# Layer-norm statistics on another engine, seven skip terms taken early, and two B tiles by transposing loads, in a one-core S5 and MLP mixer

## The chip, the cores and the metric

The kernel runs on one core of a Trainium2 chip. A time is device microseconds from launch to end of one execution. An execution that is profiled also has a span: the time from its first to its last instruction, in which the profile places everything. Kernels are compared by their medians.

A core has five engines that each work through a queue of their own in order[...]: TensorE (PE in the profile; its weight loads are shown apart as PEld), VectorE (DVE), ScalarE (ACT), GpSimd (POOL) and SyncE (SP). In this kernel SP issues loads and all transposing DMAs, POOL issues stores and accumulating DMAs.

## The reference

Input x has 2048 rows (time) of 1024 columns, in bfloat16. Cut to what matters:

```python
g = _sigmoid((x * gate_w).sum(-1, keepdims=True))
# A: a diagonal complex state space model, 1024 states
Bu = einsum("bld,pd->blp", x, B_bar)              # B_bar complex, rows p
h[t] = Lam_bar * h[t-1] + Bu[t]
a = 2.0 * einsum("blp,dp->bld", h, Cmat).real + x * Dskip
# B: layer norm, then an MLP with 3584 hidden units
y = (x - mean(x)) / sqrt(var(x) + 1e-5)
b = gelu(y @ w1 + b1) @ w2 + b2
return g * a + (1 - g) * b
```

The term of the skip that the change touches is g * x * Dskip; the statistics that it touches are the mean and the variance of each row of x.

## The kernel before

**Stages.** PE goes through four kinds of work. First the start: the first x rows and the B rows of p tiles 0 and 1 (a p tile is 128 of the 1024 states) are transposed on PE and multiplied plainly. Then the B stage, Bu: fourteen groups of 28 matmuls of 512 columns, each a block product of two by two blocks that takes seven block products in place of eight (class SG; its parts p1 to p7 are the seven products, with sums of operands made by DVE and sums of results made by ACT and DVE). Then the MLP in eight blocks: "m" blocks (x W1 and gelu, seven groups each) and "b" blocks (times W2, four groups each), over two halves of the hidden units (Fh) and two halves of the rows (c), in the order m00 b00 m01 b01 m11 b11 m10 b10. Last the y stage: eight groups of 56 matmuls, states times C, in the order of row blocks 4 5 6 0 1 2 3 7, with the final sum.

The MLP's result of the half Fh = 0 goes, already scaled by (1 - g), to a scratch tensor ACS in DRAM, one piece of 128x1024 f32 per tile k of 128 rows (L1459, a store on POOL). That of Fh = 1 is added to it by an accumulating DMA (L1461, on POOL). The y stage loads the piece back (L1527).

The state scans (L1238 to L1265, function ssm) lie on DVE beside the MLP, as work of low priority; their results go through DRAM (HS) to the y stage.

**What sets the order.** The program adds tasks to a graph with an engine, an estimated duration and a priority (small is early). A list scheduler simulates the engines with these estimates and writes down each engine's queue. A task is held back in this plan until its operands are there by the estimates: a result handed to another engine costs 0.2 us, data from a DMA 3 us more before a compute engine uses it, and a task may have further slack (the attribute slack). On the chip each engine follows the written order, waiting at each instruction for what it needs. So a change of any estimate or priority can reorder queues everywhere.

**What the change touches.**

- B rows of p tiles 2 and 3: load_b (L626 to L637) loads them plainly on SP; t_b (L657 to L678) transposes them on PE, eight transposes (L666) for each of the real and imaginary part, into PSUM, and ACT copies them out (L677). bu_plain (L963 to L983) calls t_b for tile 2 between the matmuls of tile 1, row chunk 0, and for tile 3 between those of tile 0, row chunk 1 (its argument mid). B rows of p tiles 4 to 7 come by transposing DMAs on SP already (bT_dma, L1146 to L1150). Their transposing loads must have landed before the first four stores of Bu to DRAM (u_store, L958, POOL): us_t's tasks get them as dependencies.
- x columns by row chunk of 512 rows, as PE needs them: chunk 0 is transposed on PE, chunks 1 to 3 by transposing DMAs on SP (xT_dma, L1048).
- The gate's row sums: z_gate (L1108 to L1125) multiplies all of x by two columns, gate_w and ones, in 32 matmuls (L1116), ACT copies the result out (L1124), z_move stores it (L1132, POOL) and loads it back by columns (SP). The columns are Z, for the gate, and SUM, for the means. It is called after p3 of the first group of the B stage. It must come before the fourth sum of x (ut4 of x_sums), which overwrites x chunk 1 with what p4 of that group needs.
- Layer-norm statistics: ln_stats (L1068 to L1095), called once per four tiles of 128 rows. ACT squares each tile and sums along the row (L1072); POOL computes mean, mean of squares, square of the mean, variance, its power -1/2 and mean times that (L1082 to L1087) on 128x4 columns; DVE normalizes each tile in place (L1092); the rows are stored to DRAM (L1094) and come back transposed (L1061).
- Skip terms: in the y stage y_load (L1512 to L1531) loads, for each of the 16 tiles, ACS[k] (L1527) and x (L1528) on SP; DVE multiplies x by Dskip (L1529, 128x1024 bf16) and adds g times that to the ACS piece (L1530, 128x1024 f32).
- Eviction buffers of Bu: EVS, and EVN, which gives the buffer of each of the fourteen groups.

The helper dve_tt (L940) records most two-operand additions, mm (L876 with start, L878 without) records the groups' matmuls, snap and begin (L895, L896, L905) and the seed in p1 (L912) record ACT's copies from PSUM. A seed copies the bank of p1 to the bank in which p6 goes on; between p1 and p6 lie p7 of the group before and p5.

Of the kernel before, what the change touches and what calls it, by code (L numbers as in the profile page):

```python
# [7 lines left out]
F32 = mybir.dt.float32  # L8
# [31 lines left out]
def c_tt16(N):  # L40
    return 0.07 + N / 1920.0
# [378 lines left out]
def build(nc, A_x, A_Lambda_re, A_Lambda_im, A_B_re, A_B_im, A_C_re, A_C_im, A_log_dt, A_Dskip,  # L420
# [25 lines left out]
    with es:  # L446
# [14 lines left out]

        NCOL = 660
        CST = sb("cst", [128, NCOL], F32)
# [90 lines left out]
        b_cst["MS0"] = bc("S1")  # L554
        alloc_cols("MHALF", TT)
        alloc_cols("KF", 2 * PT)
# [24 lines left out]
        def bcast(ap, off, name):  # L581
# [11 lines left out]
              reads=[v_ones], writes=[b_ident], name="ident")  # L593
        g.add("pool", 0.3, P0, lambda e: e.memset(C("MHALF", 0, TT), -0.5), writes=[bc("MHALF")], name="mhalf")

# [348 lines left out]
        b_hs = [[B("hs%d_%d" % (p, h)) for h in range(L // T)] for p in range(PT // 4)]  # L944
        EVS = [EV0, EV0 + 4096, BQ[2], SSM, SSM + 4096, SSM + 8192]
        us_t = {}
        xpose_t = {}
        EVN = (0, 1, 0, 1, 0, 1, 2, 0, 5, 1, 2, 0, 1, 2)
        US5 = B2B
# [12 lines left out]

        def bu_plain(pt, c, mid=None):  # L963

# [3 lines left out]
            for ri in range(2):  # L968
# [11 lines left out]
                if c % 2 == 1:  # L980
                    u_store(pt, c // 2, ks, q, ri)
                if mid is not None:
                    t_b(mid, (1.0, q), (ri,), (7, 3), pe_last)  # L983

# [82 lines left out]

        def ln_stats(c, prio):  # L1068
            for i in range(TT):
                k = c * TT + i  # L1070
                xv = XNAT[k]
                g.add("act", c_act(D, psum=False) + 0.15, (max(prio[0], 4.0), k), lambda e, xv=xv, k=k: e.activation(v_j.ap, xv.ap, AF.Square, accum_out=C("SSQ", k)),  # L1072
                      reads=[xv], writes=[v_j, bc("SSQ%d" % k)], name="ln_sq%d" % k, extra=[first_a[3]])
            k0 = c * TT

            def po(nm, fn, rd, wr):
                g.add("pool", 0.5, prio, fn, reads=[bc(r) for r in rd], writes=[bc(w) for w in wr], name="ln_%s%d" % (nm, c))
            invD = 1.0 / D
            sums = ["SUM%d" % (k0 + i) for i in range(TT)]
            sqs = ["SSQ%d" % (k0 + i) for i in range(TT)]  # L1080
            s = ".%d" % c
            po("mean", lambda e: e.tensor_scalar(C("MEAN", k0, TT), C("SUM", k0, TT), invD, 0.0, ALU.mult, ALU.add), sums, ["MEAN" + s])  # L1082
            po("ex2", lambda e: e.tensor_scalar(C("EX2", k0, TT), C("SSQ", k0, TT), invD, 1e-5, ALU.mult, ALU.add), sqs, ["EX2" + s])  # L1083
            po("msq", lambda e: e.tensor_tensor(C("MSQ", k0, TT), C("MEAN", k0, TT), C("MEAN", k0, TT), ALU.mult), ["MEAN" + s], ["MSQ" + s])
            po("var", lambda e: e.tensor_tensor(C("VAR", k0, TT), C("EX2", k0, TT), C("MSQ", k0, TT), ALU.subtract), ["EX2" + s, "MSQ" + s], ["VAR" + s])
            po("rstd", lambda e: e.tensor_tensor(C("RSTD", k0, TT), C("VAR", k0, TT), C("MHALF", 0, TT), ALU.pow), ["VAR" + s, "MHALF"], ["RSTD" + s])
            po("nmr", lambda e: e.tensor_tensor(C("NMR", k0, TT), C("MEAN", k0, TT), C("RSTD", k0, TT), ALU.mult), ["MEAN" + s, "RSTD" + s], ["NMR" + s])  # L1087
            for i in range(TT):
                k = k0 + i
                xv = XNAT[k]  # L1090
                o = xv
                g.add("dve", 0.35, prio, lambda e, xv=xv, k=k, o=o: e.tensor_scalar(o.ap, xv.ap, C("RSTD", k), C("NMR", k), ALU.mult, ALU.subtract),  # L1092
                      reads=[xv, bc("RSTD" + s), bc("NMR" + s)], writes=[o], name="ln_norm%d" % k)
                g.dma(prio, lambda e, k=k, o=o: e.dma_start(out=XNS[k * 128:(k + 1) * 128, :], in_=o.ap), 128 * D * 2,  # L1094
                      ssem("xns", k, True), reads=[o], writes=[b_xns[k]], name="xns%d" % k, q="sp" if k < 8 else "pool", extra=xn_t if k > 7 else ())  # L1095
# [31 lines left out]
        def z_move():  # L1127
# [8 lines left out]
            def em_ld(e):  # L1136
                return [e.dma_start(out=C(("Z", "SUM")[r], 0, NTT), in_=bass.AP(ZS.tensor, ZS.offset + r * L, [[1, 128], [128, NTT]]), allow_slow_non_contiguous=True) for r in range(2)]
            g.dma(prio, em_ld, L * 8, sem("d_zl"), reads=[b_zs[0]], writes=[bc("Z%d" % k) for k in range(NTT)] + [bc("SUM%d" % k) for k in range(NTT)], name="zl", ndma=2)

        xT_dma(1, (-0.84, 0))  # L1140
        load_b(2, (-0.83, 0))
        load_b(3, (-0.82, 0))
        xT_dma(2, (-0.4, 0))
        xT_dma(3, (-0.3, 0))

        def bT_dma(pt):  # L1146
            for ri, ap in enumerate((A_B_re, A_B_im)):
                o = AR.v(bqo(pt, 2 * ri), [(128, DT), (1, 128)])
                xpose_t[pt, ri] = g.dma((0.3, pt, ri), lambda e, o=o, ap=ap, pt=pt: e.dma_start_transpose(out=o.ap, in_=ap[pt * 128:(pt + 1) * 128, :]), 128 * D * 2,
                      ssem("bT", 2 * pt + ri), writes=[o], name="bTd%d.%d" % (pt, ri), xpose=True)  # L1150

        for c in range(2):
            for pt in range(2):
                bu_plain(pt, c, {(1, 0): 2, (0, 1): 3}.get((pt, c)))
        for k in range(4, 8):
# [11 lines left out]
        for n, (pt, pr) in enumerate(order):  # L1167
# [10 lines left out]
            cur.p6()  # L1178
            cur.p2()
            cur.p3()  # L1180
            if n == 0:
                z_gate()
                z_move()
                x_sums(0, seq[0], (1,))
                for c in range(2):
                    ln_stats(c, (2.55, c))
            if prev is not None:
# [14 lines left out]
        pb[0] = 10.0  # L1202
        for c in range(2, NCH):
            ln_stats(c, (4.0, c))

# [169 lines left out]


        HF = FT // 4

# [43 lines left out]
        def b_group(Fh, c, tp):  # L1422
# [19 lines left out]
            def fin(qd, q, bk):  # L1442
# [13 lines left out]
                if done.get(2 * t) and done.get(2 * t + 1):  # L1456
                    av = AR.v(o0[t], [(1, D)], F32)
                    if Fh == 0:
                        g.dma((10.0, q + 2), lambda e: e.dma_start(out=ACS[k], in_=av.ap), 128 * D * 4, ssem("ao", k % 4, True), reads=[av], writes=[b_acs[k]], name="acs%d.%d" % (Fh, k), q="pool")  # L1459
# [52 lines left out]
        def y_load(yi, ts=(0, 1), state=True):  # L1512
# [8 lines left out]
            for t in ts:  # L1521
                n = 2 * yi + t
                k = 2 * qb + t
                av = AR.v(AV[n % 8], [(1, D)], F32)
                xi = 0 if n < 1 else 1 + n % 4
                xv = AR.v(XV[xi], [(1, D)])
                g.dma((52.0, n), lambda e, av=av, k=k: e.dma_start(out=av.ap, in_=ACS[k]), 128 * D * 4, ssem("yac", n % 8), reads=[b_acs[k]], writes=[av], name="acl%d" % k)  # L1527
                g.dma((52.0, n), lambda e, xv=xv, k=k: e.dma_start(out=xv.ap, in_=x2[k * 128:(k + 1) * 128, :]), 128 * D * 2, ssem("yx", xi), writes=[xv], name="yx%d" % k)  # L1528
# [75 lines left out]
        for n, it in enumerate(flat):  # L1604
# [33 lines left out]
            if prev is not None:  # L1638
# [7 lines left out]
                elif kind == "m":  # L1646
                    w1_due[0] += x > 0
            if kind == "b":
                if w1_due[0]:
# [110 lines left out]
```

## Time and profile before

| | |
|---|---|
| median of 8 runs | 562.19 us (560.14 to 565.11) |
| the profiled execution | 560.14 us, the fastest of the eight |
| its span | 558.4 us |
| mean granted TensorE clock | 0.997 of full speed |
| chain that ended last, by engine | PE 87%, DVE 3%, ACT 2%, issue 2%, SP's queue 2%, POOL 1%, DMA 1% |
| moved by DMA | 125.58 MB, mean 225 GB/s |
| transposing loads of B rows (L1149) | 8, 256 KB each, 1.2 to 1.9 us of SP, 4.1 to 5.7 us from issue to landing |
| transposing loads of x (L1048) | 3, 1 MB each, 4.3 to 6.7 us of SP, 6.5 to 10.4 us from issue to landing |
| statistics on POOL (L1082 to L1087) | 24 instructions on 128x4 f32, 0.19 to 3.84 us each |
| skip terms on DVE in the y stage (L1529, L1530) | 16 tiles, mean 685 and 1278 ns |

A row of a timeline or of a group names line, engine and operation, what is written from what is read, shapes and count; brackets hold the idle time of the engine just before and what ended it. A mean duration of a pipelined engine is longer than the distance of its instructions: 512-column matmuls show 379 ns and follow one another every 216 ns; products of 128x1024 on DVE show 685 ns and follow every 600.

### The profile page before, as it was taken

Reading aid. Unit: us, or ns where it says so; the run is one execution under the profiler, and the core shown is the slowest. Engines: PE = TensorE matmul, PEld = TensorE weight load, DVE = VectorE, ACT = ScalarE, POOL = GpSimd, SP = SyncE. Lnnn points to the kernel's source line nnn. Section 1 sums busy time; section 2 is a strip of 40 time slices with the busy share of each in tenths; the row PEclk is TensorE's granted clock in tenths of the full one; section 3 lists DMA queues with packets and bytes.
Section 4 is the critical chain, followed back from the end, with each engine's and each line's share of the span. In section 5 each row is a group of like instructions: output and inputs, shape, how many; then the busy total and the mean of one; then the engine's idle time right before and its main releaser. Section 6 shows DMA issues by size and latency. Waiting matters only on the chain.

```text
span 558.4 us, 7447 instructions
## 1 busy us (share of the span) xinstructions
PE 543.4 (97%) x2576; PEld 250.2 (45%) x2623; DVE 520.2 (93%) x897; ACT 284.5 (51%) x477; POOL 101.6 (18%) x152
## 2 busy tenths in 40 slices
PE   8999999999999999999999999999999999999995
PEld 6444444444444444444444444444444444444442
DVE  3899999999999999999999999999999998999852
ACT  3998897657764356764346662347663231111110
POOL 2027916750001010001120101120001110011000
PEclk9999999999999999999999999999999999999998
DMA  9999889758757363315999997897688799898501
GB/s 249 278 199 285 294 193 306 261 185 257 226 121 263 115 225 114 109 41 163 336 343 325 333 252 197 204 228 246 199 235 166 168 309 352 286 356 307 176 38 56
DMA packets 122758, 125.58 MB, mean 225 GB/s; under 512 B 70475, under 2 KB 99929, under 8 KB 121697
## 3 DMA queue, kind: packets, MB, share of 16 engines
q1 hardware_dynamic: 110256, 79.33, 50.4%
q0 software_dynamic: 12464, 45.78, 26.3%
q8 instruction: 20, 0.33, 0.2%
q14 instruction: 18, 0.14, 0.1%
HBM read 60.98 MB, written 48.38 MB: 196 GB/s over the span
## 4 chain that ended last, share of the span: by engine, by line
PE 87%; DVE 3%; ACT 2%; issue 2%; SPq 2%; POOL 1%; DMA 1%; DVEq 0%; POOLq 0%; ACTq 0%
PE ps L878 66%; PE ps L876 20%; SPq L1048 1%; DVE ar L1252 1%; DMA ar<-in_A_B_im_dram 1%; DVE ar L940 1%; ACT ar L1072 1%; ACT ar L677 0%; DVE ar L1238 0%; POOL scr_u L958 0%; DVE ar L1370 0%; POOL cst L1083 0%; DVE ar L1039 0%; PE ps L1116 0%; DVE ar L1092 0%
## 5 line engine op out<-in xcount | busy, mean ns | idle before, releaser
L878 PE MATMUL ps<-ar 128*128 128x512 f16 (+1 forms) x1793 | 411.7, 379 | 3.3 <-ACT ps L912 1.2
L878 PEld LDWEIGHTS ps<-ar 128*128 128x128 f16 (+1 forms) x1832 | 178.9, 98 | 218.4 <-ACT ps L912 3.0
L940 DVE TENSOR_TENSOR ar<-ar 128x512 f16<-128x512 bf16 (+7 forms) x244 | 149.7, 653 | 5.7 <-ACT ar L677 2.1
L876 PE MATMUL ps<-ar 128*128 128x512 bf16 (+1 forms) x616 | 152.2, 379 | 1.7 <-DVE ar L940 1.1
L876 PEld LDWEIGHTS ps<-ar 128*128 128x128 bf16 (+1 forms) x624 | 60.6, 98 | 74.1 <-DVE ar L940 1.6
L1252 DVE TENSOR_TENSOR_SCAN ar<-cst,init,ar 128x256 bf16<-128x256 f32 x128 | 88.3, 735 | 0.4
L895 ACT ACTIVATE ar<-ps 128x512 f32<-128x512 f32 x100 | 59.1, 596 | 47.8 <-PE ps L876 35.4
L1238 DVE TENSOR_TENSOR ar<-ar 128x2048 bf16<-128x2048 bf16 x64 | 77.0, 1218 | 0.1
L912 ACT ACTIVATE ps<-ps 128x512 f32<-128x512 f32 x66 | 38.5, 583 | 66.1 <-PE ps L876 54.7
L1366 ACT ACTIVATE ar<-ps,cst 128x512 bf16<-128x512 f32 x56 | 38.4, 686 | 22.8 <-PE ps L878 22.2
L896 ACT ACTIVATE ar<-ps,cst 128x512 f32<-128x512 f32 x32 | 22.0, 688 | 44.6 <-PE ps L878 19.9
L1372 ACT ACTIVATE ar<-ar,cst 128x512 bf16<-128x512 f32 x56 | 40.0, 714 | 7.9 <-DVE ar L1370 7.9
L1449 ACT ACTIVATE ar<-ps,cst 128x512 f32<-128x512 f32 x32 | 22.0, 688 | 40.8 <-PE ps L878 40.7
L1241 DVE TENSOR_TENSOR ar<-ar 128x1024 bf16<-128x1024 bf16 x64 | 42.6, 685 | 0.1
L1370 DVE TENSOR_TENSOR ar<-ps,ar 128x512 f32<-128x512 f32 x56 | 38.3, 684 | 2.8 <-PE ps L878 2.4
L958 POOL DMA_DIRECT2D scr_u<-ar x32 | 25.0, 785 | 29.3 <-DVE ar L1034 19.0
L1551 DVE SCALAR_TENSOR_TENSOR ar<-ps,cst,ar 128x512 bf16<-128x512 f32 x32 | 23.6, 747 | 7.1 <-PE ps L878 7.0
L1459 POOL DMA_DIRECT2D scr_ac<-ar x16 | 8.6, 535 | 113.4 <-DVE ar L1452 62.6
L1461 POOL DMA_DIRECT2D scr_ac<-ar x16 | 13.8, 871 | 82.2 <-DVE ar L1452 40.8
L1452 DVE SCALAR_TENSOR_TENSOR ar<-ps,cst,ar 128x512 f32<-128x512 f32 x32 | 23.7, 742 | 1.1 <-PE ps L878 0.9
L1270 POOL DMA_DIRECT2D scr_h<-ar x16 | 9.1, 569 | 81.1 <-DVE ar L1241 74.4
L1558 POOL DMA_DIRECT2D out_dram<-ar x14 | 7.6, 546 | 82.9 <-DVE ar L1551 82.9
(118 smaller groups left out, 269.7 us busy)
## 6 DMA issues: line engine op xcount, KB each, us to landing
scr_ac<-ar POOLq DMA_DIRECT2D x32, 512.0 KB, 6.0
ar<-in_B_w_dram SPq DMA_DIRECT2D x21, 512.0 KB, 5.2
ar<-in_A_x_dram SPq DMA_DIRECT2D x32, 256.0 KB, 4.8
scr_u<-ar POOLq DMA_DIRECT2D x32, 256.0 KB, 4.8
ar<-scr_u SPq DMA_DIRECT2D x16, 512.0 KB, 4.7
scr_h<-ar POOLq DMA_DIRECT2D x16, 512.0 KB, 5.9
ar<-scr_h SPq DMA_DIRECT2D x8, 1024.0 KB, 7.9
ar<-scr_ac SPq DMA_DIRECT2D x16, 512.0 KB, 7.5
```

The lines of the kernel that those rows point to most:

```text
L876: ins = e.matmul(V(PS[bk], 0, [(1, n)]), st[i].ap, mv[i].ap, start=(i == 0), stop=(i == K - 1))
L878: ins = e.matmul(V(PS[bk], 0, [(1, n)]), st[i].ap, mv[i].ap, start=False, stop=(i == K - 1), skip_group_check=True)
L895: return e.activation(o.ap, V(PS[bk], 0, [(1, 512)]), AF.Copy)
L912: g.add("act", c_act(512), (pb[0], q - 2), lambda e: e.activation(V(PS[b], 0, [(1, 512)]), V(PS[a], 0, [(1, 512)]), AF.Copy), reads=[b_ps[ ...
L940: g.add("dve", c_tt16(n), (pr or pb[0], q), lambda e: e.tensor_tensor(o.ap, a.ap, b.ap, op), reads=[a, b], writes=[o], name=nm, extra=ex). ...
L958: us_t[pt, pr, ri] = g.dma((1.0, q), lambda e: e.dma_start(out=US[pt // 4, :, 4 * pr:4 * pr + 4, r0:r0 + T], in_=evv.ap), 2 * 128 * CH * 2 ...
L1238: g.add("dve", c_tt16(UE), pri(i), lambda e: e.tensor_tensor(o.ap, a.ap, tbl.ap, ALU.mult), reads=[a, tbl], writes=[o], name=nm + tag)
L1241: g.add("dve", c_tt16(UE // 2), pri(i), lambda e: e.tensor_tensor(o.ap, a.ap, b.ap, op), reads=[a, b], writes=[o], name=nm + tag)
L1252: lambda e, pt=pt, ri=ri, vin=vin, go=go: e.tensor_tensor_scan(go.ap, Cb("R", pt, T), vin.ap, V(INIT, pt * 2 + ri, [(1, 1)]), ALU.mult, AL ...
L1366: g.add("act", c_act(512, ap_operands=1), (10.0, q + 1), lambda e: e.activation(o.ap, V(PS[bk], 0, [(1, 512)]), AF.Gelu_apprx_tanh, bias=C ...
L1370: g.add("dve", c_dve(512), (10.0, q - 2), lambda e: e.tensor_tensor(sv.ap, V(PS[bk], 0, [(1, 512)]), sv.ap, ALU.add), reads=[b_ps[bk], sv] ...
L1372: g.add("act", c_act(512, psum=False, ap_operands=1), (10.0, q + 3), lambda e: e.activation(o.ap, sv.ap, AF.Gelu_apprx_tanh, bias=C("B1", ...
```

## The change

It does several things at once. The statistics are computed for eight tiles in one set, not for four: two calls in place of four. In the first set (priority below 3) all but the power go to DVE, with an estimate of 0.09 us each; the second stays on POOL. The load that brings back the gate's sums gets 4 us of slack. The B rows of p tiles 2 and 3 come by transposing loads on SP, tile 2 ahead of x chunk 2 and tile 3 between chunks 2 and 3, and bu_plain has no transposes between its matmuls. The gate's matmuls and what follows from them come in the second group of the B stage, between p6 and p2, not at the end of the first. A seventh eviction buffer joins. And the skip terms of tiles 0 to 6 leave the y stage: in the first m block for tiles 0 to 2 and in the second for tiles 3 to 6 x is loaded, multiplied by Dskip on DVE, scaled by g in two halves on ACT and written to ACS by a DMA on POOL: a plain store for tiles 0 to 2, whose MLP result is then accumulated, and an accumulating one for tiles 3 to 6.

The diff, cut to its core:

```diff
-        EVS = [EV0, EV0 + 4096, BQ[2], SSM, SSM + 4096, SSM + 8192]
+        EVS = [EV0, EV0 + 4096, BQ[2], SSM, SSM + 4096, SSM + 8192, W1R]
-        EVN = (0, 1, 0, 1, 0, 1, 2, 0, 5, 1, 2, 0, 1, 2)
+        EVN = (0, 1, 0, 1, 0, 1, 2, 0, 5, 6, 0, 1, 2, 0)
...
-        def bu_plain(pt, c, mid=None):
+        def bu_plain(pt, c):
...
-                if mid is not None:
-                    t_b(mid, (1.0, q), (ri,), (7, 3), pe_last)
...
-        def ln_stats(c, prio):
-            for i in range(TT):
+        def ln_stats(c, prio, m=1):
+            nt = m * TT
+            for i in range(nt):
...
             def po(nm, fn, rd, wr):
-                g.add("pool", 0.5, prio, fn, reads=[bc(r) for r in rd], writes=[bc(w) for w in wr], name="ln_%s%d" % (nm, c))
+                g.add(*(("dve", 0.09) if prio[0] < 3 and nm != "rstd" else ("pool", 0.5)), prio, fn, reads=[bc(r) for r in rd], writes=[bc(w) for w in wr], name="ln_%s%d" % (nm, c))
...
-            g.dma(prio, em_ld, L * 8, sem("d_zl"), reads=[b_zs[0]], writes=[bc("Z%d" % k) for k in range(NTT)] + [bc("SUM%d" % k) for k in range(NTT)], name="zl", ndma=2)
+            g.dma(prio, em_ld, L * 8, sem("d_zl"), reads=[b_zs[0]], writes=[bc("Z%d" % k) for k in range(NTT)] + [bc("SUM%d" % k) for k in range(NTT)], name="zl", ndma=2).slack = 4.0
 
         xT_dma(1, (-0.84, 0))
-        load_b(2, (-0.83, 0))
-        load_b(3, (-0.82, 0))
+        bT_dma(2, (-0.83, 0))
+        bT_dma(3, (-0.35, 0))
         xT_dma(2, (-0.4, 0))
         xT_dma(3, (-0.3, 0))
...
-                bu_plain(pt, c, {(1, 0): 2, (0, 1): 3}.get((pt, c)))
+                bu_plain(pt, c)
...
             cur.p5()
             cur.p6()
-            cur.p2()
-            cur.p3()
-            if n == 0:
+            if n == 1:
                 z_gate()
                 z_move()
                 x_sums(0, seq[0], (1,))
-                for c in range(2):
-                    ln_stats(c, (2.55, c))
+                ln_stats(0, (2.55, 0), 2)
+            cur.p2()
+            cur.p3()
...
-        for c in range(2, NCH):
-            ln_stats(c, (4.0, c))
+        ln_stats(2, (4.0, 2), 2)
...
+        EARLY = {k: blk for blk, ks in enumerate(([0, 1, 2], [3, 4, 5, 6])) for k in ks}
+        v_de = AR.v(AO, [(1, D)])
+
+        def d_load():
+            g.dma((48.0, 0), lambda e: e.dma_start(out=v_de.ap, in_=bass.AP(A_Dskip.tensor, A_Dskip.offset, [[0, 128], [1, D]])), 128 * D * 2, ssem("dske", 0), writes=[v_de], name="dske")
+
+        def skip_term(k):
+            ox = AO + (2048 + 2048 * (k % 4) if EARLY[k] else 6144 + 2048 * (k % 2))
+            og = AO + 10240 + 4096 * (k % 2)
+            xv, xg = AR.v(ox, [(1, D)]), AR.v(og, [(1, D)], F32)
+            g.dma((48.0, k), lambda e: e.dma_start(out=xv.ap, in_=x2[k * 128:(k + 1) * 128, :]), 128 * D * 2, ssem("xe", k % 4), writes=[xv], name="yx%d" % k)
+            g.add("dve", c_tt16(D), (49.0, k), lambda e: e.tensor_tensor(xv.ap, xv.ap, v_de.ap, ALU.mult), reads=[xv, v_de], writes=[xv], name="xd%d" % k)
+            for h in range(2):
+                xh_, gh = AR.v(ox + h * 1024, [(1, 512)]), AR.v(og + h * 2048, [(1, 512)], F32)
+                g.add("act", c_act(512, psum=False, ap_operands=1), (49.0, k, h), lambda e, xh_=xh_, gh=gh: e.activation(gh.ap, xh_.ap, AF.Copy, scale=C("G", k)), reads=[xh_, bc("G")], writes=[gh], name="xg%d.%d" % (k, h))
+            if k // 8 < EARLY[k]:
+                g.dma((49.0, k), lambda e: e.dma_start(out=ACS[k], in_=xg.ap, accum_op=ALU.add), 128 * D * 4, ssem("xg", k % 2, True), reads=[xg, b_acs[k]], writes=[b_acs[k]], name="xgs%d" % k, q="pool")
+            else:
+                g.dma((49.0, k), lambda e: e.dma_start(out=ACS[k], in_=xg.ap), 128 * D * 4, ssem("xg", k % 2, True), reads=[xg], writes=[b_acs[k]], name="xgs%d" % k, q="pool")
...
-                    if Fh == 0:
+                    if Fh == 0 and (k not in EARLY or k // 8 < EARLY[k]):
...
+                if k in EARLY:
+                    continue
...
+            if kind == "m" and Fh == 0:
+                ks = [k for k in EARLY if EARLY[k] == c]
+                if x == 0:
+                    d_load()
+                elif x < 5:
+                    for k in ks[(x - 1) * len(ks) // 4:x * len(ks) // 4]:
+                        skip_term(k)
```

## Prediction

> **What bounds the kernel now.** I read the busy shares first, then the stages, then what TensorE waited for, then the first 35 us instruction by instruction.
>
> Busy time of each engine, from the first part of the page:
>
> ```profile
> PE 543.4 (97%) x2576; PEld 250.2 (45%) x2623; DVE 520.2 (93%) x897; ACT 284.5 (51%) x477; POOL 101.6 (18%) x152
> ```
>
> PE is busy for 543.4 of 558.4 us, so only PE's own work and its 15 us of idle time can be won. DVE, at 93%, is close behind. By stages (length, then busy time of PE, PEld, DVE, ACT, POOL, then clock, DMA share, GB/s):
>
> ```profile
> 13.50:24.00 10.50, 9.60 (x68) 5.31 (x70) 8.45 (x29) 9.11 (x16) 0.00 (x0) 1.00 1.16 268
> 24.00:34.00 10.00, 9.55 (x68) 3.96 (x68) 9.97 (x62) 9.82 (x19) 0.78 (x2) 1.00 1.17 222
> 34.00:115.00 81.00, 80.68 (x371) 36.51 (x375) 80.33 (x161) 65.73 (x124) 47.92 (x63) 1.00 0.94 265
> 115.00:125.00 10.00, 9.05 (x42) 4.01 (x42) 9.76 (x21) 5.74 (x10) 7.37 (x6) 1.00 0.50 161
> ...
> 305.00:312.00 7.00, 5.82 (x28) 2.47 (x27) 6.72 (x13) 4.28 (x8) 0.53 (x1) 1.00 0.95 290
> 312.00:448.00 136.00, 135.37 (x620) 61.69 (x631) 133.67 (x195) 66.23 (x106) 15.53 (x21) 1.00 0.87 222
> 448.00:552.00 104.00, 103.09 (x472) 46.74 (x478) 89.32 (x123) 16.32 (x28) 10.79 (x18) 1.00 0.72 244
> ```
>
> From 34 to 552 us PE runs at its pace, 0.216 us per 512-column matmul, apart from two holes of about 1 us each. The rest of its idle time is in the first 34 us and in the last 7 (the last addition and stores, which the change leaves alone). The y stage, 448 to 552, has no hole. PE's waits after 115 us:
>
> ```profile
> 121.66 3.63 PE L878 MATMUL ps<-ar 128*128 128x512 f16 x16 [0.90 <-ACT ps L912]
> 309.61 1.04 PE L876 MATMUL ps<-ar 128*128 128x512 f16 x4 [1.12 <-DVE ar L940]
> ```
>
> Now the start, PE by time (start, us, idle before it in brackets); L666 are the transposes of B rows:
>
> ```profile
> 13.73 1.67 PE L876 MATMUL ps<-ar 128*128 128x512 bf16 x7 [0.16 <-ACT ar L978]
> 16.10 0.62 PE L666 MATMUL ps<-ident,ar 128*128 128x128 bf16 x8 [0.69 <-DMA ar<-in_A_B_im_dram]
> 16.56 1.89 PE L876 MATMUL ps<-ar 128*128 128x512 bf16 x8
> 18.28 0.61 PE L666 MATMUL ps<-ident,ar 128*128 128x128 bf16 x8
> ...
> 28.71 2.76 PE L878 MATMUL ps<-ar 128*128 128x512 f16 x12 [0.29 <-ACT ps L912]
> 31.40 1.90 PE L1116 MATMUL ps<-ar,gwc 128*2 128x512 bf16 x32
> ```
>
> The four groups of eight transposes that go are at 16.10, 18.28, 20.46 and 22.63, and the matmuls behind start 0.45 us later each. SP's queue in the same stretch:
>
> ```profile
> 4.56 6.67 SPq L1048 DMA_TRANSPOSE ar<-in_A_x_dram  x1
> 11.28 0.57 SPq L634 DMA_DIRECT2D ar<-in_A_B_re_dram  x1
> ...
> 14.24 9.08 SPq L1048 DMA_TRANSPOSE ar<-in_A_x_dram  x2
> 23.37 2.00 SPq L622 DMA_DIRECT2D ar<-in_A_x_dram  x4
> 25.42 1.44 SPq L1149 DMA_TRANSPOSE ar<-in_A_B_re_dram  x1
> ```
>
> SP issues without a pause until 45 us, and the DMA share is over 0.9, so whatever is put into this queue delays all that follows.
>
> [...]each group has an ACT copy (L677, 1.0 us). [...]in this stream eight cost 0.45 us. [...]256 KB take SP 1.6 us transposed (L1149) against 0.43 plain (L634/L635). [...]four-column statistics on POOL take 0.19 to 3.84 us while DVE is full. [...]here they are on POOL, 0.87 us each (L1461) against 0.54 plain (L1459).
>
> **The change, part by part.**
>
> *Transposes off PE.* Removed: 4 x 0.45 = 1.80 us of PE, on the path since nothing else bounds PE there. The wait of 0.69 us for the B rows goes too. What is late next is the x chunk 1: issued at 4.56, and with the longest landing time of its line, 10.4 us, there at 15.0; its first use moves from 18.73 to 17.2, so it is in time. ACT loses four copies of about 0.9 us and so reaches the seed of the first group less late; of the waits of 0.29 and 0.16 us there I count 0.3 as won. Sum: -2.8 us. The B stage then starts (first group, tile 2) at about 24.1 in place of 26.5.
>
> *What the transposing loads cost.* SP: four plain issues (2.8 us from 11.28 to 14.24) give way to four transposing ones of 1.6, and the pair of tile 3 goes between x chunks 2 and 3. From 11.28: tile 2 to 14.5, x2 to 19.0, tile 3 to 22.3, x3 to 26.9, in place of 23.3. So everything behind (x tiles 4 to 7, B tiles 4 to 7, x tiles 8 to 11, the gate's return load) is about 3.5 us later. Tile 2 lands about 4.6 us after issue, at 17.5, needed at 24.1; tile 3 at 25, needed at 28.4; x3 at 22.3 + 7.2 = 29.5 (32.7 with 10.4), needed by the gate's matmuls, which move behind p6 of the second group, at 32. B tile 4 is needed at 60 and lands by 47. All covered, x3 barely: taken at 0; 0 to +0.7 as bounds. Below nothing is excluded here, since nothing waits less.
>
> *The gate moved.* It keeps its 32 matmuls (1.9 us). But the sum that overwrites x chunk 1 (128x2048, 1.14 us on DVE) must follow it and precede p4 of the first group, with only p2 and p3 (1.73 us) between; before, a whole group lay there. With two handovers it just fits if DVE is free at that moment; DVE is full there (9.97 of 10.00). I take +0.3, bounds 0 and +1.5. Behind the sum on DVE are the second group's additions, for which PE's banks wait.
>
> *Statistics.* 24 small POOL instructions become 7; five of 0.16 us, 0.8 us, go to DVE. On POOL they cost no PE time before, so there is nothing to win. New is that DVE, which works in order, waits for the gate's return load and then for POOL's power (1.0 to 1.8 us). Before, that load was issued at 41.0 and POOL went on at 50.4; 3.5 us later that is 53.9. The added slack of 4 us in the plan moves DVE's first instruction back by as much, so I expect a wait of 0 to 2 us, hidden behind about 2 us of buffered work: 0, bounds 0 and +3. Behind it are the B stage's additions. In the second set, eight norms (0.46 us apart) follow one another at about 100 us where four stood; 1.9 us more at once: 0, bound +0.9. Its stores free two of the four w1 slots some 14 us later, to about 108, with the data used at 124: covered. The new eviction buffer lies in a third slot, whose load must wait for a store of about 85 to 90 us and is used at 112: covered too.
>
> *Early skip terms.* Seven tiles: the product by D (0.60 us on DVE) moves from the y stage to the first two m blocks; the scaled addition (1.20 us, 8.4 in all) leaves DVE; ACT gets 14 copies at 0.7 (nearest row L1372, 0.71), 10 us in two stages (114 to 157 and 199 to 242) where it is busy some 70%; POOL gets 7 more DMAs and 3 of its plain ones become accumulating, 6 us on an engine at 18%. SP gets the seven x loads earlier, and D twice. The y stage has no hole for DVE to fill, so this wins 0. In the m blocks a copy of 0.7 in front of a seed lies within the seed's slack (p7 and p5, 1.73 less 0.6). 0; bounds -0.5 (a lighter DVE in a stage with no hole) and +6 (the rival below). State scans come up to 5 us later; the last but one unit ends at 434, its state is needed at 471: covered.
>
> *The two holes* at 121 and 309 come of the order of DVE's queue, which the planner writes anew: they may go (-2.0), stay, or grow (+1). Taken as staying.
>
> Sum: -2.8 + 0.3 = -2.5. The profiled execution took 560.14 us (span 558.4 and 1.7 around it), so it would take 557.6. It was the fastest of eight, whose median is 562.19; the same difference gives 559.7.
>
> **Rivals.**
>
> *Both holes go too.* For: both holes are DVE delays (the chain of waits leads through scans and additions). Against: DVE is as full as before. -2.5 - 2.0 = -4.5: 557.7.
>
> *The start gives it back.* x3 lands as late as 10.4 us after issue, the sum behind the gate finds DVE taken, and the first u stores, held on POOL until all B loads have landed, come 3.5 us later. 0.7 + 1.5 on top: about -0.6: 561.6. It is also the case in which the change doesn't do what it says: waits for loads replace the transposes.
>
> *Slower: ACT stands behind the skip terms.* The scaled copies wait on ACT for DVE's product; behind them stand the seeds. A precedent is at 121: ACT waited 1.54 us for a DVE addition, the seed came late, and PE lost 0.90. If each of seven tiles does this: 6.3 us, -2.5 + 6.3 = +3.8: 566.0. It outweighs the gain from three such events on. Against: ACT waited eleven times for such additions and only once did PE lose by it.
>
> **How the numbers follow.** Chances: forecast 0.46, both holes go 0.21, start gives it back 0.17, slower 0.16. Half a per cent, 2.8 us, is about what a measurement can tell from no change. The forecast lies close to it (559.4): a little over half of its chance counts as faster, with all but nothing of the second case missing: 0.25 + 0.21 = 0.46 faster; the rest of it, the third case and a little of the fourth, 0.39, within; 0.15 slower. The range runs from 557.0 (-2.8, both holes, and the -0.5 of the skip terms: -5.3) to 564.5, inside the slower case (six events of seven would be 565.1): about a tenth is left out above, less below.
>
> **What would show it.** Right: no L666 after 13.5 us; the first L878 matmul of the B stage at about 26 in place of 28.71; the loads of B tiles 4 to 7 ending on SP near 42; PE busy time down by about 2; ACT and DVE waits in the m blocks as before. Wrong: PE waiting for x or B loads between 24 and 36; a DVE hole of several us near 50; PE waits on ACT L912 repeated from 121 to 150 and from 205 to 235.

## The result, and the profile after

| | before | after |
|---|---|---|
| median | 561.44 us (559.83 to 565.11, 32 runs) | 567.96 us (564.94 to 569.92, 11 runs) |
| profiled execution, its span | 560.14, 558.4 us | 566.34, 564.6 us |
| mean granted TensorE clock | 0.997 | 0.992 |

The changed kernel takes 1.0104 times as long, 95% interval 1.0081 to 1.0126. The medians differ by 6.5 us, where 2.5 us less was forecast; the time is above the forecast range.

Line numbers move: the transposing B loads are now L1143, the gate's return load L1136, the statistics L1081 to L1086, the norms L1091, the state scans L1235 to L1249, their store L1267, the state loads of the y stage L1535, its ACS and x loads L1543 and L1548.

Busy times, from the first part of the page of after:

```profile
PE 544.5 (96%) x2544; PEld 249.3 (44%) x2591; DVE 513.3 (91%) x895; ACT 289.1 (51%) x487; POOL 95.5 (17%) x142
```

There are 32 PE instructions fewer, as the diff says (the transposes), and DVE is 7 us less busy. Yet PE's busy time is up by 1.1 us. Instructions left out that don't lower the busy time are a hint that others became slower.

The start, PE by time, of after:

```profile
13.24 12.03 PE L876 MATMUL ps<-ar 128*128 128x512 bf16 x54 [0.16 <-ACT ar L978]
26.00 2.76 PE L878 MATMUL ps<-ar 128*128 128x512 f16 x12 [0.73 <-ACT ps L912]
...
36.29 1.02 PE L878 MATMUL ps<-ar 128*128 128x512 f16 x4 [0.41 <-DVE ar L940]
```

One row of 54 matmuls stands where transposes cut the stream four times, and there is no wait for B rows. SP's queue in after, the start and the gate's return load:

```profile
12.10 2.31 SPq L1143 DMA_TRANSPOSE ar<-in_A_B_im_dram  x1
...
43.68 6.33 SPq L1136 DMA_DIRECT2D cst<-scr_z  x2
```

PE's waits from 60 us on in after, all that its timeline shows:

```profile
67.77 1.90 PE L878 MATMUL ps<-ar 128*128 128x512 bf16 x8 [1.95 <-DVE ar L940]
120.90 3.63 PE L878 MATMUL ps<-ar 128*128 128x512 f16 x15 [0.29 <-ACT ps L912]
326.55 1.04 PE L878 MATMUL ps<-ar 128*128 128x512 f16 x4 [0.18 <-DVE ar L1367]
455.75 6.87 PE L878 MATMUL ps<-ar 128*128 128x512 f16 x31 [0.83 <-DVE ar L1470]
478.77 3.19 PE L876 MATMUL ps<-ar 128*128 128x512 bf16 x7 [4.07 <-DMA ar<-scr_h]
```

The last one is new and in the stage that had no hole before. It is the load of the states (HS) for the third group of the y stage. The start of this group in before, and the row behind the hole in after:

```profile
475.38 1.89 PE L876 MATMUL ps<-ar 128*128 128x512 bf16 x8
...
481.76 2.99 PE L878 MATMUL ps<-ar 128*128 128x512 f16 x8
```

In before there is no wait. In after the seven matmuls of the row at 478.77 are followed by the next row at 481.76: one every 427 ns, not every 216. The stretches around it in after (length, busy time of PE, PEld, DVE, ACT, POOL, then clock, DMA share, GB/s):

```profile
474.00:479.00 5.00, 0.93 (x5) 0.38 (x4) 5.00 (x8) 0.00 (x0) 1.09 (x2) 0.81 0.82 291
479.00:483.00 4.00, 4.00 (x10) 1.37 (x9) 4.00 (x6) 0.58 (x1) 0.00 (x0) 0.50 0.99 376
```

The granted clock is 0.50 after the hole. This is also why PE's busy time rose.

**Where the time went.** PE can be followed by its position: the same matmul in both traces, after minus before.

| place | after - before, us |
|---|---|
| second group of the B stage starts (28.61; before, 33.46 less 1.9 for the gate's matmuls that came first) | -2.95 |
| third group (37.15; 39.28), behind gate and sum | -2.13 |
| 69.5, behind the wait of 1.95 | 0.0 |
| behind the hole at 121 (0.29, was 0.90; 120.90; 121.66) | -0.76 |
| where the hole of 1.12 was, which is gone (307.55; 309.61) | -2.06 |
| second y group (462.46; 463.29), behind waits of 0.18 and 0.83 | -0.83 |
| third y group (478.77; 475.38) | +3.39 |
| its second part (484.58; 478.83), behind the slow matmuls | +5.75 |
| end of PE (557.28; 551.53) | +5.75 |

The start won what was forecast, and the wait near 68 took it back. The two small holes of before, one shorter and one gone in after, then won 2.1, of which the waits at 326 and 455 left 0.8. One place, the third y group, costs 6.6 us: 4.2 of waiting and 2.4 of half clock.

**What the load waited for.** The state scans run in 16 units; each ends with a store to HS. Before, the store of the last unit but one, which holds the third y group's states, and the load (POOL and SP rows of the timeline of before):

```profile
434.25 0.56 POOL L1270 DMA_DIRECT2D scr_h<-ar  x1 [1.73 <-DVE ar L1241]
...
458.36 0.33 SPq L1517 DMA_DIRECT2D ar<-scr_h  x1
```

The same rows of after:

```profile
459.81 0.56 POOL L1267 DMA_DIRECT2D scr_h<-ar  x1
469.66 0.41 SPq L1535 DMA_DIRECT2D ar<-scr_h  x1
```

The store is 25.6 us later. In before the state had landed at 471.38, 4.0 us before PE began. In after the store lands 9.2 us after issue (the DMA part for 440 to 485 us), at 469.0; on SP two x loads end at 469.55; then the load goes out. The chain of waits of after goes on:

```profile
469.66 8.66 DMA ar<-scr_h
478.32 0.45 issue
478.77 3.19 PE ps L876 x7
```

So from the store to PE it takes 9.2 + 0.65 + 8.66 + 0.45 = 19.0 us. PE is due there 12.1 us after the second y group starts (475.38 less 463.29 in before). The store must therefore be out about 6.9 us before the second y group starts. Call this distance the lead. Before it was 463.29 - 434.25 = 29.0, after it is 462.46 - 459.81 = 2.65: short by 4.2, and the hole is 4.07. (That is the same wait read from its other end, not a second measurement; the durations of the two DMAs are those of this run.)

### The profile page after: what moved, and what is told of

It is laid out like the page before. It is cut to its first block, busy times and chain, and to the rows that moved or that the text cites. A ratio compares the mean times of both kernels' runs of the same rounds, so it can differ in the third digit from the quotient of the medians.

```text
span 564.6 us, 7409 instructions
## 1 busy us (share of the span) xinstructions
PE 544.5 (96%) x2544; PEld 249.3 (44%) x2591; DVE 513.3 (91%) x895; ACT 289.1 (51%) x487; POOL 95.5 (17%) x142
## 4 chain that ended last, share of the span: by engine, by line
PE 79%; DVE 9%; DMA 5%; issue 3%; ACT 2%; POOL 1%; SPq 0%; DVEq 0%
PE ps L878 60%; PE ps L876 19%; DVE ar L940 2%; DMA ar<-in_B_w_dram 2%; DMA scr_ac<-ar 2%; DMA ar<-scr_h 2%; DVE ar L816 1%; DVE ar L1367 1%; DVE ar L1091 1%; DVE ar L1550 1%; ACT ar L1071 1%; PE ps L704 0%; DVE ar L654 0%; ACT ar L978 0%; DVE ar L1571 0%
## 5 line engine op out<-in xcount | busy, mean ns | idle before, releaser
L878 PE MATMUL ps<-ar 128*128 128x512 f16 (+1 forms) x1799 | 413.5, 380 | 6.3 <-DVE ar L940 2.4
L878 PEld LDWEIGHTS ps<-ar 128*128 128x128 f16 (+1 forms) x1832 | 178.8, 98 | 223.7 <-issue 3.2
L940 DVE TENSOR_TENSOR ar<-ar 128x512 f16<-128x512 bf16 (+7 forms) x244 | 149.6, 653 | 6.2 <-DMA scr_ac<-ar 2.6
L1249 DVE TENSOR_TENSOR_SCAN ar<-cst,init,ar 128x256 bf16<-128x256 f32 x128 | 89.2, 737 | 0.3
L1235 DVE TENSOR_TENSOR ar<-ar 128x2048 bf16<-128x2048 bf16 x64 | 77.1, 1218 | 0.1
L912 ACT ACTIVATE ps<-ps 128x512 f32<-128x512 f32 x66 | 38.5, 583 | 71.8 <-PE ps L876 66.2
L1479 POOL DMA_DIRECT2D scr_ac<-ar x19 | 16.4, 882 | 115.4 <-DVE ar L1470 33.1
L1470 DVE SCALAR_TENSOR_TENSOR ar<-ps,cst,ar 128x512 f32<-128x512 f32 x32 | 23.8, 743 | 1.9 <-PE ps L878 0.8
L1569 DVE SCALAR_TENSOR_TENSOR ar<-ar,cst 128x512 f32<-128x512 f32 x16 | 12.0, 748 | 10.8 <-ACT ar L895 10.8
L1026 ACT ACTIVATE ar<-ps 128x512 bf16<-128x512 f32 x28 | 16.6, 595 | 9.1 <-PE ps L878 8.8
```

Of the source, the lines that this page charges most:

```text
L878: ins = e.matmul(V(PS[bk], 0, [(1, n)]), st[i].ap, mv[i].ap, start=False, stop=(i == K - 1), skip_group_check=True)
L912: g.add("act", c_act(512), (pb[0], q - 2), lambda e: e.activation(V(PS[b], 0, [(1, 512)]), V(PS[a], 0, [(1, 512)]), AF.Copy), reads=[b_ps[ ...
L940: g.add("dve", c_tt16(n), (pr or pb[0], q), lambda e: e.tensor_tensor(o.ap, a.ap, b.ap, op), reads=[a, b], writes=[o], name=nm, extra=ex). ...
L1235: g.add("dve", c_tt16(UE), pri(i), lambda e: e.tensor_tensor(o.ap, a.ap, tbl.ap, ALU.mult), reads=[a, tbl], writes=[o], name=nm + tag)
L1249: lambda e, pt=pt, ri=ri, vin=vin, go=go: e.tensor_tensor_scan(go.ap, Cb("R", pt, T), vin.ap, V(INIT, pt * 2 + ri, [(1, 1)]), ALU.mult, AL ...
```

## The experiments

The theory after the result: the re-planned DVE queue finishes that unit too late, and this alone makes the change slower. The rivals: the early skip terms cost by themselves; the statistics or their late data cost, near 68 us; the B loads cost. Three parts are taken alone, in pairs and together. B stands for the B loads, the gate's move and the seventh buffer, S for the statistics (with the slack of the return load), K for the early skip terms. Ratios of the experiments are to the kernel before on the same chip, where its median was 563.2 to 563.5 us.

### Each part alone, and the change without K

skip_only is before with K:

```diff
+            if kind == "m" and Fh == 0:
+                ks = [k for k in EARLY if EARLY[k] == c]
...
+                        skip_term(k)
```

> The kernel before with the early skip terms alone. Theory: the early products delay DVE's state scans so far that the state of the third y group (row block 6) is stored after about 445 us and its load lands too late: PE waits in the y stage, up to 4 us with a drop of the granted clock behind it, 563 to 567 us; nothing changes in the first 110 us. Rival (the scans are late because PE's start is earlier, not because of the skip terms): no hole in the y stage, 561 to 562 us.

Measured: 1.0053 (1.0037 to 1.0070), 565.95 us. The time is as expected, the reason is not: there is no hole in the y stage; the lead is 9.94. PE waits 1.00 and 1.03 near 69 and 75, 0.89 at 125, 0.50 at 158, 0.87 at 289 and 0.88 together from 320 to 329.

stats_only is before with S:

```diff
-                for c in range(2):
-                    ln_stats(c, (2.55, c))
+                ln_stats(0, (2.55, 0), 2)
```

> The kernel before with the statistics of the change alone (sets of eight, the first on DVE but for the power, 4 us of slack on the return load), and the gate where it was. Theory: the eight norms come in one lump between 58 and 68 us and a group's operand sums stand behind them, so PE waits about 2 us once near 65: 563 to 564 us; y stage as before. Rival (the wait at 67.8 us comes of the earlier start of PE): no wait there, 561 to 562 us.

Measured: 1.0017 (1.0003 to 1.0032). The wait of 2 us near 65 did not come; waits of 0.96 at 74 and 1.47 at 288 are the largest. The lead is 30.0.

bload_only is before with B:

```diff
-        load_b(2, (-0.83, 0))
-        load_b(3, (-0.82, 0))
+        bT_dma(2, (-0.83, 0))
+        bT_dma(3, (-0.35, 0))
...
-            if n == 0:
+            if n == 1:
                 z_gate()
```

> The kernel before with the transposing loads of B tiles 2 and 3, the later gate and the seventh eviction buffer alone; statistics in sets of four on POOL, no early skip terms. Theory: the start is 2.9 us earlier, 0.5 to 0.9 is lost behind the gate, no 2 us wait at 68, and no hole in the y stage: 558.5 to 560 us. Rival (the earlier start alone makes the scans late): a hole of 2 us or more at the third y group, 561 to 565 us.

Measured: 1.0078 (1.0046 to 1.0110), some 8 us above what was expected, its runs widely spread (562.57 to 570.98, and one of 574.6 that the ratio leaves out). The part that wins 2.95 us at the start has the highest ratio of the three when alone. The profile is of one of its longer executions (570.78 us, median 567.86). Its largest waits, PE in bload_only:

```profile
68.38 1.05 PE L876 MATMUL ps<-ar 128*128 128x512 f16 x4 [4.35 <-DVE ar L940]
```

and 3.79 at 518.67, behind DVE as well; the second I can't explain. DVE in bload_only, the norms just before the first of them:

```profile
62.80 2.62 DVE L1091 TENSOR_SCALAR ar<-ar,cst 128x1024 bf16<-128x1024 bf16 x5 [3.01 <-POOL cst L1086]
```

With the statistics left on POOL, DVE waits 3.01 us for POOL's last one, and the operand sums behind the norms come late. POOL began that chain at 55.44, when the gate's sums had returned, and one of its products (L1083) took 4.11 us. PE's wait isn't always that long: in bload_skip below, with the statistics on POOL as well, it is 2.38. So it isn't shown that moving the statistics to DVE is what shortens this wait.

after_noskip is the change without K:

```diff
-        EARLY = {k: blk for blk, ks in enumerate(([0, 1, 2], [3, 4, 5, 6])) for k in ks}
+        EARLY = {}
```

> The changed kernel without the early skip terms; everything else of the change stays. Theory: no hole of 4 us at the third y group, the waits near 36 and 68 us stay: 560.5 to 562.5 us. Rival (scans late by the earlier start or the statistics): the hole stays, 565 us or more.

Measured: 0.9979 (0.9965 to 0.9992). The wait near 68 is still there, 2.35. The y stage has no hole, lead 9.93. The unit's last product on DVE, then two accumulating DMAs of POOL, the store and the load:

```profile
447.10 0.68 DVE L1238 TENSOR_TENSOR ar<-ar 128x1024 bf16<-128x1024 bf16 x1
...
452.55 1.73 POOL L1479 DMA_DIRECT2D scr_ac<-ar  x2 [8.93 <-DVE ar L1238]
453.88 0.95 POOL L1267 DMA_DIRECT2D scr_h<-ar  x1
466.23 0.33 SPq L1535 DMA_DIRECT2D ar<-scr_h  x1
```

DVE has done the unit at 447.78, 16.0 us before the second y group, and its store stands 6.1 us behind the two DMAs in POOL's queue. The load of the state goes out 12.35 us after the store and 9.67 us before PE starts the third group; in after load and start lie 9.11 us apart.

B and S together are faster than before, though each alone is slower. The parts don't add up, so none of them has a price of its own.

### The hole in the y stage

after_yorder computes row block 6 one group later. Ahead of the y stage the work stands in the same order: the traces of the two kernels have the same sequence on DVE, ACT and POOL until 469 us and on SP until 452:

```diff
-        YORD = (4, 5, 6, 0, 1, 2, 3, 7)
+        YORD = (4, 5, 0, 6, 1, 2, 3, 7)
```

> The changed kernel with the y groups in the order 4 5 0 6 1 2 3 7 in place of 4 5 6 0 1 2 3 7, so that row block 6, whose state is stored last but one, is due one group (12 us) later. Theory (the hole at the third y group is a late scan): the hole of 4.1 us and the 1.7 us of lowered clock behind it go, 561 to 563.5 us, the wait near 68 us stays. Rival (SP's queue holds the state loads behind loads that wait for the accumulating stores of the last MLP block): a hole of 2 us or more at the third or fourth y group stays, 565 us or more.

Measured: 0.9964 (0.9949 to 0.9979), 1.4% below the change. The unit is stored at 460.96 with the same lead of 2.65; the hole of 4 us and the half clock are gone (granted clock 1.00 from 460 to 500). Left in the y stage are these two waits and one of 0.51 at 494 (PE in after_yorder):

```profile
475.32 1.90 PE L878 MATMUL ps<-ar 128*128 128x512 f16 x8 [1.19 <-DVE ar L1571]
...
489.93 1.90 PE L876 MATMUL ps<-ar 128*128 128x512 bf16 x8 [0.62 <-DMA ar<-scr_h]
```

1.4% is 7.9 us. The hole, the half clock and the 0.83 us at 455, which is gone too, make 7.4, and the three new waits take 2.3 back. From the first L878 matmul of the B stage to the start of the last y group PE takes 515.8 us in after, 510.5 in this trace and 508.4 in that of after_yorder_noslack (below), which has none of the new waits: 5.3 and 7.4 us less. This settles the main point: one state load that came too late is what turned a gain into a loss.

after_noprod asks which piece of K moves the unit: only the seven products on DVE are gone (the skip term of those tiles is then g times x), all loads, ACT copies and stores stay.

```diff
-            g.add("dve", c_tt16(D), (49.0, k), lambda e: e.tensor_tensor(xv.ap, xv.ap, v_de.ap, ALU.mult), reads=[xv, v_de], writes=[xv], name="xd%d" % k)
```

> The changed kernel without the seven early products by Dskip on DVE (so the skip term of tiles 0 to 6 is g times x; left out are 7 x 0.6 us of DVE and nothing else). Theory (the scans are late by DVE's own time): the last but one scan unit is stored near 454 us as without the skip terms, no hole of 4 us at the third y group, 561 to 563.5 us. Rival (the skip terms hurt by their loads, stores and ACT copies): unit stored after 458 us, hole stays, 566 us or more.

Measured: 0.9965 (0.9955 to 0.9976). Lead 9.87, no hole in the y stage; the wait near 69 is 2.38. So ACT's copies, POOL's DMAs and SP's loads of K don't make the hole; 4.2 us of products on DVE are what moves the unit over the edge.

### The wait near 68

Each kernel with B has it. The theory was that the gate's sums come back late, since SP issues the return load 2.7 us later and takes 6.33 us for it, not 4.33. after_zfirst puts that load ahead of the x loads of tiles 8 to 11:

```diff
-        for k in range(8, 12):
-            load_x(k, (0.5, k))
...
+                for k in range(8, 12):
+                    load_x(k, (1.0, seq[0], k))
+                    g.tasks[-1].deps.add(zl_t[0])
```

> The changed kernel with the gate's return load put ahead of the loads of x tiles 8 to 11 on SP. Theory (the wait near 68 us is the late return load, which lands at 55 us in place of 50, through the statistics and the eight norms): it lands near 51, the 2 us wait goes, -2 us against the changed kernel plus what the planner's new order does to the y hole: 562 to 566 us. Rival (the wait comes of the eight norms in one lump): the wait of about 2 us stays, 566 to 568 us.

after_zfirst_yorder has both edits:

> The two edits together: return load ahead of x tiles 8 to 11, and y groups in the order 4 5 0 6 1 2 3 7. Theory: the 2.9 us of the start minus 0.9 behind the gate remain and both new waits go: 558.5 to 560.5 us, faster than the kernel before. Rival (new waits take the place of these): 562 us or more.

Measured: 1.0041 (1.0026 to 1.0055) and 1.0049 (1.0034 to 1.0064). The load took 2.36 us of SP and the wait fell to 0.46, as the theory had it, but not for its reason: DVE did its first statistic (L1081) at 59.72, and in after at 59.70, where the sums had been there since about 55.4. DVE gets to the statistics when its written queue does, not when the data comes. What shortened the wait I take to be the new order of the queue around them; no run isolates it. PE gained little: the matmul behind the wait starts at 67.52, in after at 67.77. In exchange there are new waits: 0.80 at 115, 1.43 at 153, 1.11 at 288. My time for the pair, 558.5 to 560.5, was missed by 5 us. It is a useful control, too: after_zfirst's lead is 9.70, it has no hole in the y stage, and there the other order of groups wins nothing.

before_again is the kernel before, unchanged, for a second profile.

> The kernel before once more, for a profile of another execution: the one profiled first was the fastest of its eight. Theory: an ordinary execution has, with the same queues, one or two waits of about 1 us between 65 and 76 us that the first profile doesn't show[...]; they account for most of the 2 to 3 us between the fastest and the median. Rival: the difference is only in the first 15 us, in the landing of the first loads.

Measured: 563.35 us, span 561.6. PE in before_again:

```profile
69.29 1.90 PE L878 MATMUL ps<-ar 128*128 128x512 bf16 x8 [0.80 <-ACT ar L895]
74.92 3.69 PE L878 MATMUL ps<-ar 128*128 128x512 f16 x16 [1.14 <-ACT ps L912]
```

The profile that I predicted from has neither wait. It was the fastest of eight runs. This one, with the same queues and a time near the median, loses 1.94 us near 70, as much as the change does. So the wait of 1.95 in after is a loss against the first profile and, as far as one more profile can tell, hardly against the median.

### The other pairs, and the slack

bload_skip is the change with the old statistics and no slack (B and K):

```diff
-                ln_stats(0, (2.55, 0), 2)
+                for c in range(2):
+                    ln_stats(c, (2.55, c))
```

> The changed kernel with the statistics as before (four sets of four, all on POOL, no slack). Theory (DVE's statistics shorten the late chain behind the return load): the wait near 68 us is 4 us in place of 2, and the last but one scan unit, three products less late in the plan, leaves no hole of 4 us at the third y group: 563 to 567 us. Rival (the statistics do harm, as more work on DVE): the wait near 68 us is gone and the time is under 562 us.

Measured: 0.9987 (0.9976 to 0.9999); the median of 563.01 is at the low edge of what was expected. Lead 9.87, no y hole; a wait of 2.38 at 66.5, not the 4 us that were expected and not the 4.35 of B alone.

stats_skip is before with S and K, both edits as shown.

> The kernel before with the statistics and the early skip terms, B tiles 2 and 3 on PE as before. Theory (each of the two costs a few small waits and the big hole needs the earlier start): no hole of 4 us in the y stage, 564 to 567 us, about what the skip terms alone cost. Rival (the skip terms make the hole whatever the start): a hole of 3 us or more at the third y group, 568 us or more.

Measured: 1.0030 (1.0020 to 1.0039). Lead 9.65, no y hole; waits of 1.16 at 73 and 1.49 at 288.

after_yorder_noslack takes the return load's slack out of after_yorder:

```diff
-            g.dma(prio, em_ld, ..., name="zl", ndma=2).slack = 4.0
+            g.dma(prio, em_ld, ..., name="zl", ndma=2)
```

> The changed kernel with the y order 4 5 0 6 1 2 3 7 and without the 4 us of slack on the return load; in the queues this moves one x load from ahead of the return load to behind it and nothing else. Theory (every microsecond of the return load counts near 68 us): the load lands 0.7 us earlier, the wait near 68 us is shorter by up to that, 560.5 to 561.5 us. Rival (DVE comes to the mean later than the load anyway): no difference from the y order alone, 561.5 us, within 0.1 per cent.

Measured: 0.9969 (0.9938 to 0.9999), six runs, no different from after_yorder; the wait near 67 is 1.29, there 1.30. No effect of the slack shows.

### All of them by the place of one unit

Counting in DVE's written queue how many of the 32 MLP additions of the b blocks (L1470) stand ahead of the unit's last product shows three places, and nothing between:

| kernels | additions ahead | lead, us | state load goes out before PE is due, us | hole at the third y group | ratio |
|---|---|---|---|---|---|
| before, S | 27 | 29.0, 30.0 | 17.0, 17.0 | no | 1, 1.0017 |
| K | 30 | 9.94 | 9.7 | no | 1.0053 |
| B | 30 | 9.93 | 9.7 | no | 1.0078 |
| S and K | 30 | 9.65 | 9.7 | no | 1.0030 |
| B and K | 30 | 9.87 | 9.5 | no | 0.9987 |
| B and S | 30 | 9.93 | 9.7 | no | 0.9979 |
| the change without the products | 30 | 9.87 | 9.8 | no | 0.9965 |
| the change, return load first | 30 | 9.70 | 9.7 | no | 1.0041 |
| the same, other y order | 30 | 9.70 | group moved | no | 1.0049 |
| B, S and K: the change | 32 | 2.65 | 4.9 | 4.07 | 1.0104 |
| the change, other y order | 32 | 2.65 | group moved | no (0.62 at the fourth) | 0.9964 |
| the same without slack | 32 | 2.65 | group moved | no | 0.9969 |

The needed lead of 6.9 holds for the DMA times of after. In the seven kernels with a lead of 9.65 to 9.94 whose third group takes the unit the load goes out 12.0 to 12.4 us after the store, not 9.85 as in after, and 9.5 to 9.8 us before PE is due. With the 9.11 us (8.66 + 0.45) from load to PE of after, 0.4 to 0.7 us would be left (an estimate): all seven stand close to the hole. In these, and in the eighth, the lead isn't DVE's alone either. DVE ends the unit 14.0 to 16.0 us before the second y group, and the store stands 4 to 6 us in POOL's queue behind the accumulating DMAs; in before and in after it goes out 0.3 us after DVE's product. The only kernel with a lead under 6.9 that asks for the unit in the third group has the hole.

## Why the prediction was wrong

**The failed step** is "State scans come up to 5 us later; the last but one unit ends at 434, its state is needed at 471: covered". I took the DVE time that is added (4.2 us of products) as the time by which the scans move. The scans are what the plan puts in when nothing more urgent is ready, on an engine that is full: before that point, DVE in after is busy 138.9 of 143 us from 305 to 448. Work put ahead of them takes the free places, and the next free place for a whole unit may be a stage later. The first unit's store was 5.4 us later (116.2, was 110.8), those in the middle 10 to 19, the last but one 25.6 where up to 5 was forecast. Either of B and K alone moves it by three additions and its lead from 29.0 to 9.9, of which 13 to 14 us are DVE's and the rest is the store's place in POOL's queue. The second error is in the same sentence: 471 was when the state had landed in before, which is not the latest time at which the unit may end; two DMAs, in after 9.2 and 8.66 us, lie between the store and PE. And a hole of 4 us cost 6.6, which no term had.

**Other steps, in their order.**

- *Transposes off PE, -2.8*: right. The second group of the B stage starts 2.95 us earlier; the first L878 matmul of the B stage is at 26.00 (about 26 was forecast), and the last L666 begins at 12.34.
- *Transposing loads on SP, 0*: right. No PE wait for x or B; the B loads end at 40.1 on SP (42 was forecast). In before they hold SP longer than plain loads of the same 256 KB (1.2 to 1.9 us, plain 0.43 in the median) but land as soon: 4.1 to 5.7 us after issue, plain x tiles 4.8 in the median.
- *The gate, +0.3*: the mechanism was right, 0.8 measured (-2.95 to -2.13), inside its bounds; the wait of 0.41 for L940 is the sum behind the gate.
- *Statistics, 0 with +3 as bound*: 1.95 us near 68 against the profile, inside the bound. The reason was not the forecast one: DVE waited 0.36 us for POOL, and an earlier return load left the statistics where they were. In the chain of waits of after the power on POOL (1.76 us) and the eight norms in a row (3.98) stand ahead of this wait. The eight norms of the second set (100.2 to 104.1) led to no PE wait.
- *Early skip terms, 0*: right for ACT, POOL and SP, wrong for the scans behind DVE.
- *The two holes, taken as staying*: the first fell to 0.29 and the second went, by position -0.6 and -1.3. The rival "both holes go" was right on this and covered by the other loss.
- *The slower rival, ACT behind the skip terms*: no repeated waits for L912 came. The sign of that rival came true by another mechanism. My chance for a slower kernel, 0.15, was too small since I had listed only one way for re-planned queues to lose, and let DVE's delay of the scans off with a sentence.
- *The sum* of -2.5, 0.44% of 562.19, stands close to what is measured once the y hole is taken out: after_yorder's 0.9964, and 0.9965 without the products. In part that is luck. Against the profile that I predicted from, the wait near 68 spends the whole gain (0.0 at 69.5) and the two lost holes, which I had taken as staying, win some of it again; against the median it counts for less, since the kernel before has such waits there too.

What stays open: K alone costs 3.0 us, of which its waits of 0.50, 0.87 and 0.88, less the hole of 1.12 at 309 that went, explain 1.1. The place of each remaining wait of 0.3 to 2.4 us differs from kernel to kernel with the written queue. I can't give a cause for each, only that nearly all of them end on DVE or on ACT behind it. Why the planner's list puts the unit at 27, 30 or 32 was read from the queues, not derived.

## What to carry to other kernels

Low-priority work on a full engine moved by stages here when work was added ahead of it (the last unit but one by 25.6 us), not by the time that was added (4.2 us of products): find its last deadline, subtract every DMA on the way to the user, and compare that lead with a shift of a whole stage. Take the DMAs as slow as they are in that stretch: the same store landed in 5.8 us in before and 9.2 in after, and in seven kernels between them the load followed the store by 12. A cheap repair is to use the late result later; here a swap of two groups turned 1.0104 into 0.9964, the lowest ratio of the kernels tried (0.9965 and 0.9969 are no different). When a re-planned kernel gets slower, try the parts in pairs as well: two parts that each lose alone can win together, so single ablations say little about which of them is at fault.

## What the runs showed of the hardware

**One hole cost PE twice.** In after the hole of 4.07 us began at 474.70. The granted clock was still 1.00 when 2.45 us of it had passed, 0.50 from 477.15 to 483.97, and 1.00 again behind that. At half clock one matmul followed another every 427 ns, and 2.4 us were lost on top of the wait. In bload_only a lower clock followed the holes of 4.35 and 3.79 us as well (0.86 from 68 to 80, 0.83 from 516 to 526). Two shorter holes differ: in after_noskip the clock was 1.00 from 66 to 72, around 2.35 us, but in after_noprod it was 0.72 from 68 to 74, around 2.38. The length of a hole doesn't tell these two apart, and no run shows what does.

**A small load can hold a queue.** The gate's return load is two DMAs of columns; they took SP 4.33 us in before, 6.33 in after and 2.36 in after_zfirst, where a plain load of an x tile took 0.43 in the median (before). And one 128x8 product on POOL (L1083) took 4.06 us in after and 0.21 in after_noskip. In after it began at 55.80, and the stores behind it, which stand ahead of the power of the first set in the chain to the wait near 68, went out at 59.81; no run tells what of that wait is due to it.
